# Layer two's output projection by pairs of tiles in seven products, and the copied sums made a stage earlier

## The chip, the cores and the metric

The kernel runs on one core of a Trainium2 chip. The core has a matrix engine (PE in the profile; its weight loads have a row of their own, PEld), a vector engine (DVE), a scalar engine (ACT), a general engine (POOL) and a queue engine (SP) that issues most of the transfers. Sixteen DMA engines carry the transfers, whoever issues them. Matmuls write to PSUM, which has eight banks of 128 partitions by 512 fp32 values; all else is held in SBUF or in DRAM.

The metric is the device time of one execution, in microseconds (us). The text calls the matrix multiplications of a 128 by 128 weight block with a block of up to 512 columns "matmuls", and gives their width in columns.

## What is computed

The input is x, 2048 rows of 512 values. Two layers of the same form follow each other; each has an attention block A and a gated block B, both with a layer norm before them and a residual sum behind:

```python
x = x + _A_ref(_layernorm(x), A_wqkv, A_wo)      # linear attention, 32 heads
x = x + _B_ref(_layernorm(x), B_w_in, B_w_sp, B_b_sp, B_w_out)
x = x + _A_ref(_layernorm(x), A_wqkv, A_wo)
x = x + _B_ref(_layernorm(x), B_w_in, B_w_sp, B_b_sp, B_w_out)

def _B_ref(x, w_in, w_sp, b_sp, w_out):
    z = gelu(x @ w_in)                            # 2048 x 1792
    z1, z2 = z[:, :896], layernorm(z[:, 896:])
    g = w_sp @ z2 + b_sp[:, None]                 # w_sp: 2048 x 2048
    return (z1 * g) @ w_out                       # w_out: 896 x 512
```

All of it is fp32. Where the kernel multiplies, it splits each operand into a high part, rounded to the matrix engine's fp32r type, and a low part, the rest; a product is then three matmuls: high by high, high by low, low by high.

## The kernel before

One program does both layers (L = 0 and L = 1); engine queues run in the order in which the kernel's text issues instructions (a manual schedule), and semaphores make each instruction wait for what it reads and overwrites. SBUF is handed out in named slots: 22 pages (`pg`, 128 by 512), 6 quads (`qd`, 2048 columns), 4 bigs (`bg`, 3584 columns) and sixteen z tiles; PSUM in 8 banks. A slot that is given back goes to the end of a queue, and its next user waits for the last reader.

Each layer has three classes. **P1** reads the rows in 16 tiles of 128, normalises them, turns them by a store to DRAM (`xt`) and a load back, and makes the projections K and Q and the attention sums. **P2** finishes attention, adds the residual, stores x, and makes gelu(x @ w_in), z2 in the z tiles and z1 in DRAM. **P4** multiplies by w_sp, gates with z1, and multiplies by w_out.

P4's product with w_sp is cut by Strassen-like sums into seven parts, done in the order P2, P1, P6, P7, P4, P5, P3. A part has eight steps; a step splits 128 by 1024 values of w_sp or of sums of w_sp into high and low (`wsp`: ACT L932, then DVE L933) and runs 18 or 24 matmuls of width 512 (L1098 to L1100). Layer one's P4 and layer two's P2 and P4 are divided once more, into seven products with two steps each (14 steps of 12 matmuls). Sums of w_sp blocks for the divided parts lie in DRAM (`hP`). They are made by transfers alone (`Sums.halve`): a copy by SP's queue (L835) and an accumulating transfer by POOL's queue (L839), 32 in all. The first 16 (numbers 0 to 15, for "P4") are issued in layer one's P4, one a step, at steps g = 10 to 25 (its parts P1, P6 and the first two steps of P7). The other 16 (numbers 16 to 31, for layer two's "P2") are issued in layer two's P1: eight copies in its steps s = 2 to 9, eight accumulating transfers in its steps s = 6 to 13.

The result g of the spatial product stands in the four bigs, transposed: feature block f (seven of 128) by 512 rows. When a part has finished a block, `evac` (DVE) moves it from PSUM and `gate` multiplies it by z1 in place, on POOL (L1136). z1 comes back from DRAM by loads that run three ahead (`ask`).

The output stage is `for i in range(NT)` at the end of `P4.run`. For each of 16 row tiles it makes seven blocks of 128 by 128 high and low (`zsplit`: ACT L127 and DVE L130, 128 by 896 values), then 21 matmuls of width 512 (`o`, through `mm3` at L141 to L143) into one bank, adds the bank to the residual x that was loaded from DRAM (DVE L1206) and stores the sum (L1208). The high and low parts of w_out are made in P3 (`wpiece`, one of seven blocks of 128 by 512 a step), in the z tiles that P3 no longer needs.

Of the kernel before, what the change touches and what calls it, by code (L numbers as in the profile page):

```python
# [11 lines left out]
F32R = mybir.dt.float32r  # L12
AF = mybir.ActivationFunctionType
OP = mybir.AluOpType

P = 128
# [3 lines left out]
NT = S // P  # L20
NCHK = S // 512
NF = FH // P
HF = FH // 2
HT = NT // 2
# [28 lines left out]
DIVIDED = (("P4",), ("P2", "P4"))  # L53


class Sheets:


# [16 lines left out]
def mixer_kernel(ctx: ExitStack, tc: tile.TileContext, x_in, wqkv, wo_d, win1_d, win2_d, wsp_d, bsp_d, wout_d,  # L75
                 ident_d, mask_d, out_d):
    nc = tc.nc
    consts = ctx.enter_context(tc.tile_pool(name="consts", bufs=1))
    main = ctx.enter_context(tc.tile_pool(name="main", bufs=1))
# [5 lines left out]
    pages = Slots(main, "pg", 22)  # L85
# [20 lines left out]
    nc.vector.memset(mhalf, -0.5)  # L106

    xs = {(0, i): x_in[i * P:(i + 1) * P, :] for i in range(NT)}
    for st in (1, 2, 3):
        for i in range(NT):  # L110
            xs[st, i] = dram.tile(PAGE, F32, name=f"x{st}_{i}")
    for i in range(NT):
        xs[4, i] = out_d[i * P:(i + 1) * P, :]
    z1s = {}

    def load(ap, slots=pages):
        t = slots.get(PAGE)
        nc.sync.dma_start(t, ap)
        return t

    def behind(ins, other):

        tc.add_manual_dep(ins.ins, other.ins.name, mybir.DependencyInfo(
            mybir.DependencyClass.Sync, mybir.DependencyReason.DATA))

    def high(h, src):
        nc.scalar.activation(h, src, AF.Copy)  # L127
# [153 lines left out]
    class P1:  # L281
# [181 lines left out]
        def run(self, sums):  # L463
            side = deque([self.win2] * NF)
            ND = NT - DEFER
            for s in range(1, NT + 2):
                self.loadx(s + 3)
                self.turn.load(s + 1)
                if 2 <= s < NT:
                    self.T_high(s)  # L470
                if s == 1:
                    if not self.kb:
                        self.K(0)
                    self.K(1)
                elif 2 < s <= NT:
                    self.K(s - 1)
                self.ln_a(s + 2)
                if 2 <= s < NT:
                    self.T_low(s)
                if s <= NT:  # L480
                    self.K_phi(s - 1)
                if s <= ND:
                    self.Q(s - 1)
                if s == NT + 1:
                    self.late()
                if s <= NT:
# [386 lines left out]
    class P4:  # L873
# [8 lines left out]
        def __init__(self, p2, sums):  # L882
            self.L = p2.L
            self.p2, self.sums = p2, sums
            self.raw, self.w, self.z, self.z1, self.x, self.zs = {}, {}, {}, {}, {}, {}
            self.div = DIVIDED[self.L]
            self.steps = []
            for p in self.ORDER:
                if p in self.div:
                    self.steps += [(p, 2 * r + q) for r in range(7) for q in range(2)]  # L890
                else:
                    self.steps += [(p, k) for k in range(HT)]
            self.tmp, self.bank = {}, {}
            self.made = 0
# [244 lines left out]
        def evac(self, p):  # L1139

            V, bs = nc.vector, self.bs
            gates = []
            for j in range(2):
# [55 lines left out]
        def o(self, i):  # L1199
# [10 lines left out]
            if i % 4 == 3:  # L1210
                bigs.put(self.gb[i // 4])

        def zahead(self, g):

            while self.zmade <= g:
                self.zsum(self.zmade + 1)
                self.zpart(self.zmade)
                self.zmade += 1

        def run(self, nxt):  # L1220
# [16 lines left out]
            for g in range(n):  # L1237
# [11 lines left out]
                    self.evac(p)  # L1249
                    self.sp(g + 2)  # L1250
                self.sums.tick()
                if nxt is not None and 10 <= g < 26:
                    self.sums.halve(g - 10, self.mark)
                if g == 3 and not self.div:
                    self.loadb()
                if p in self.div:
# [8 lines left out]
                    self.ask(3)  # L1265
                self.tick()
                if p == "P3":
                    if k < NF:
                        self.wpiece(k)
                    if k == 6:  # L1270
                        self.loadx(0)
                        self.loadx(1)
                    if k == 7:
                        self.zsplit(0)
                if p == "P7" and k == HT - 1 and self.div:
                    self.sp(g + 3)
                if k == HT - 1 and not evac_first:
                    self.evac(p)
# [76 lines left out]
```

## Time and profile before

| | us |
|---|---|
| median of three executions | 1381.27 |
| the three executions | 1381.01, 1381.27, 7891.05 |
| the profiled execution, its own time | 1382.98 |
| its span, from the first to the last instruction | 1381.2 |
| PE busy in the span | 1371.3 |
| layer two's part P3, about | 1268.5 to 1301.2 |
| layer two's output stage, about | 1301.2 to 1377.4 |

A row of the profile that describes a group of instructions names the line in the kernel, the engine, the operation, what is written and read, the shape and the count; behind the bar stand the busy time in us and the mean duration of one in ns, and then the idle time of the engine ahead of them and what ended it. A row of a timeline begins with the start and the duration in us, and x3 means that three such instructions are merged. A row of windows has for each engine the busy time in that stretch and, in brackets, the number of instructions begun. Matmuls overlap each other's fill and drain, so a matmul's recorded duration is longer than the distance to the next one; this text calls that distance the spacing.

### The profile page before, as it was taken

The page shows a single profiled execution, that of the slowest core. Times are in us where ns is not written, and L with a number is a line of the kernel's source. Part 1 is how long each engine was busy: PE and PEld are TensorE (multiplying, and loading weights), DVE is VectorE, ACT ScalarE, POOL GpSimd, SP SyncE. Part 2 cuts the span into 40 slices and gives each one's busy share as a digit, 9 for nine tenths or more (in the row PEclk, how much of TensorE's full clock was granted, in tenths as well). Part 3 has the DMA queues.
Part 4 walks back from the last instruction along what each step waited for, and adds up shares of the span by engine and source line. Part 5 has one row for each costly group of instructions (what it writes and reads, how often), then busy time and mean ns, then how long its engine had stood idle before and what let it go on. Part 6 is the DMA issues. An engine that isn't in the chain of part 4 may idle for free.

```text
span 1381.2 us, 17464 instructions
## 1 busy us (share of the span) xinstructions
PE 1371.3 (99%) x6158; PEld 1144.6 (83%) x6158; DVE 914.2 (66%) x1371; ACT 599.8 (43%) x919; POOL 418.6 (30%) x506
## 2 busy tenths in 40 slices
PE   9999999999999999999999999999999999999998
PEld 7888888888888888888888778888888888888887
DVE  6665877753575689684566658775437768887732
ACT  5764534434332364251366545433345333643410
POOL 3753355543441300351023434432100022023500
PEclk9999999999999999999999999999999999999999
DMA  5873268775986956453648932564346444464432
GB/s 179 267 242 93 92 193 271 247 241 187 346 281 223 269 162 205 138 194 125 226 138 235 234 102 92 169 189 161 121 130 207 150 164 150 152 192 152 160 123 91
DMA packets 149977, 251.91 MB, mean 182 GB/s; under 512 B 12545, under 2 KB 51201, under 8 KB 149633
## 3 DMA queue, kind: packets, MB, share of 16 engines
q1 hardware_dynamic: 147584, 242.40, 53.9%
q0 software_dynamic: 2304, 8.39, 3.3%
q8 instruction: 48, 0.79, 0.2%
q14 instruction: 41, 0.33, 0.1%
HBM read 182.85 MB, written 84.67 MB: 194 GB/s over the span
## 4 chain that ended last, share of the span: by engine, by line
PE 95%; DMA 3%; DVE 1%; ACT 1%; issue 0%; SPq 0%; ACTq 0%; DVEq 0%
PE bank L141 19%; PE bank L143 19%; PE bank L142 19%; PE bank L1100 12%; PE bank L1099 12%; PE bank L1098 12%; DMA pg<-xt 1%; DMA qd<-s 1%; PE bank L229 1%; PE bank L558 1%; PE bank L569 0%; DMA xt<-pg 0%; PE bank L441 0%; DVE qd L933 0%; DVE bg L1153 0%
## 5 line engine op out<-in xcount | busy, mean ns | idle before, releaser
L1098 PE MATMUL bank<-qd,pg 128*128 128x512 f32 x776 | 302.0, 389 | 0.5 <-ACT pg L970 0.5
L1100 PE MATMUL bank<-qd,pg 128*128 128x512 f32 x776 | 302.1, 389 | 0.0
L1099 PE MATMUL bank<-qd,pg 128*128 128x512 f32 x776 | 302.0, 389 | 0.0
L933 DVE TENSOR_TENSOR qd<-qd,qd 128x1024 fp32r<-128x1024 f32 x130 | 166.3, 1280 | 124.2 <-ACT qd L932 123.8
L1136 POOL TENSOR_TENSOR bg<-bg,pg 128x512 f32<-128x512 f32 x56 | 104.9, 1883 | 400.3 <-ACT qd L932 330.2
L932 ACT ACTIVATE qd<-qd 128x1024 fp32r<-128x1024 f32 x130 | 137.2, 1056 | 178.0 <-PE bank L1100 121.3
L1098 PEld LDWEIGHTS bank<-qd,pg 128*128 128x128 f32 x776 | 145.7, 188 | 31.2 <-ACT pg L970 0.9
L1099 PEld LDWEIGHTS bank<-qd,pg 128*128 128x128 f32 x776 | 145.7, 188 | 30.8 <-DVE qd L933 0.4
L1100 PEld LDWEIGHTS bank<-qd,pg 128*128 128x128 f32 x776 | 145.7, 188 | 30.3 <-DVE pg L972 0.5
L143 PE MATMUL bank<-qd,pg 128*128 128x512 f32 x384 | 150.0, 391 | 0.0
L217 ACT ACTIVATE pg<-pg,nb,rs 128x512 f32<-128x512 f32 x63 | 51.1, 812 | 177.0 <-POOL nb L211 176.5
L208 POOL TENSOR_SCALAR rs<-mv 128x1 f32<-128x1 f32 x96 | 27.3, 285 | 331.7 <-DVE mv L206 325.7
L141 PE MATMUL bank<-qd,pg 128*128 128x512 f32 x288 | 112.6, 391 | 0.4 <-DVE pg L130 0.4
L142 PE MATMUL bank<-qd,pg 128*128 128x512 f32 x288 | 112.3, 390 | 0.0
L141 PE MATMUL bank<-bg,qd 128*128 128x448 f32 x256 | 94.1, 368 | 0.7 <-ACT qd L127 0.7
L142 PE MATMUL bank<-bg,qd 128*128 128x448 f32 x256 | 93.6, 366 | 0.0
L143 PE MATMUL bank<-bg,qd 128*128 128x448 f32 x256 | 93.5, 365 | 0.1
L143 PE MATMUL bank<-qd,bg 128*128 128x512 f32 x224 | 87.4, 390 | 0.0
L142 PE MATMUL bank<-qd,bg 128*128 128x512 f32 x224 | 87.4, 390 | 0.0
L141 PE MATMUL bank<-qd,bg 128*128 128x512 f32 x224 | 87.2, 389 | 0.0
L141 PE MATMUL bank<-wo,qd 128*128 128x512 f32 x224 | 87.1, 389 | 0.0
L142 PE MATMUL bank<-wo,qd 128*128 128x512 f32 x224 | 87.1, 389 | 0.0
(136 smaller groups left out, 2598.8 us busy)
## 6 DMA issues: line engine op xcount, KB each, us to landing
qd<-s SPq DMA_DIRECT2D x64, 512.0 KB, 3.6
qd<-in_wsp_dram SPq DMA_DIRECT2D x42, 512.0 KB, 4.2
pg<-x SPq DMA_DIRECT2D x64, 256.0 KB, 3.0
z<-pg SPq DMA_DIRECT2D x56, 256.0 KB, 2.8
pg<-z SPq DMA_DIRECT2D x56, 256.0 KB, 4.1
x<-pg SPq DMA_DIRECT2D x48, 256.0 KB, 2.6
pg<-in_wsp_dram SPq DMA_DIRECT2D x48, 256.0 KB, 4.8
s<-pg SPq DMA_DIRECT2D x48, 256.0 KB, 4.2
```

The source lines that it names most:

```text
L141: nc.tensor.matmul(out, ah, bh, start=start, stop=False)
L142: nc.tensor.matmul(out, ah, bl, start=False, stop=False)
L143: nc.tensor.matmul(out, al, bh, start=False, stop=stop)
L208: nc.gpsimd.tensor_scalar(rs, mv[:, 1:2], LN_EPS, None, op0=OP.add)
L217: nc.scalar.activation(y, x, AF.Identity, bias=nb, scale=rs)
L229: nc.tensor.transpose(b[:, c, :], src[:, c * P:(c + 1) * P], ident)
L932: self.mark = nc.scalar.activation(w[:, 0], r, AF.Copy)
L933: nc.vector.tensor_sub(w[:, 1], r, w[:, 0].bitcast(F32))
L1098: m(out, h[:, o], w[:, 0, j, :], start=start, stop=False, skip_group_check=True)
L1099: m(out, h[:, o], w[:, 1, j, :], start=False, stop=False, skip_group_check=True)
L1100: m(out, l[:, o], w[:, 0, j, :], start=False, stop=stop, skip_group_check=True)
L1136: behind(nc.gpsimd.tensor_tensor(u, u, z1, op=OP.mult), self.mark)
```

## The change

Layer two's output stage is replaced; layer one's stays. The new stage, `out7`, takes row tiles in pairs. With the six feature blocks 0 to 5 in two groups of three, the pair's rows are a 2 by 2 block matrix (tile by group), w_out's rows and column halves (256 wide) are another, and their product is made by seven products instead of eight (`omul`, 9 matmuls of width 256 each). Feature block 6 is multiplied as before (`olone`: six matmuls of width 256 and three of width 512). Partial sums are combined in PSUM: ACT copies one bank's half into another (three copies of 256 columns a pair) and DVE adds a copied part twice, and later matmuls accumulate on top. The sums of the left operand are made by DVE in the bigs (`osum`, four of 128 by 384), its high and low parts by ACT and DVE (`ohigh`, `olow`: 384, 768, 256 and 1536 columns), one pair ahead. Sums and splits of w_out are made in P5 and P3 (`wseven`).

For the first seven pairs the residual isn't loaded: P2's x is stored straight to the output tensor (`xs[3]` is now `xs[4]`), ACT copies the finished banks to pages, and POOL issues an accumulating transfer into the output (`ofinish`). The last pair is added on DVE and stored by SP (`olast`).

In layer two the gates with f > 2 of the first two row chunks, and those with f > 3 of the others, run on DVE instead of POOL. Of P3's last results one half is moved from PSUM before the output stage, the other half behind the first pair's work. The copied and accumulated sums 16 to 31 move from layer two's P1 to layer one's P4: seven copies at the even steps of its divided part P4, one at its last step, and the eight accumulating transfers at the steps of P5.

```diff
+FIRST = 6
+PARTS = {("P1", k): k - 2 for k in range(2, 8)} | {("P6", k): 6 + k for k in range(8)}
+PARTS |= {("P7", 0): 14, ("P7", 1): 15} | {("P4", 2 * k): 16 + k for k in range(7)}
+PARTS |= {("P4", 13): 23} | {("P5", k): 24 + k for k in range(8)}
...
-        xs[4, i] = out_d[i * P:(i + 1) * P, :]
+        xs[3, i] = xs[4, i] = out_d[i * P:(i + 1) * P, :]
...
-                elif 2 <= s < 10:
-                    sums.halve(14 + s, None)
-                if self.L == 1 and 6 <= s < 14:
-                    sums.halve(18 + s, self.mark)
...
-            behind(nc.gpsimd.tensor_tensor(u, u, z1, op=OP.mult), self.mark)
+            if self.L == 1 and f > 2 and (n < 2 or f > 3):
+                nc.vector.tensor_mul(u, u, z1)
+            else:
+                behind(nc.gpsimd.tensor_tensor(u, u, z1, op=OP.mult), self.mark)
...
+        def omul(self, parts, r, out, start, stop):
+            h, l, q = parts
+            for f in range(3):
...
+                m(out, A, x, start=start and f == 0, stop=False, skip_group_check=True)
+                m(out, A, y, start=False, stop=False, skip_group_check=True)
+                m(out, B, x, start=False, stop=stop and f == 2, skip_group_check=True)
...
+        def ofinish(self, i, *parts):
+            y = pages.get(PAGE)
+            for b, c in parts:
+                nc.scalar.activation(y[:, c], b, AF.Copy)
+            nc.gpsimd.dma_start(xs[4, i], y, accum_op=OP.add)
+            pages.put(y)
+
+        def olast(self, i, b, c):
+            x = self.x[i]
+            nc.vector.tensor_add(x[:, c], x[:, c], b)
+            nc.sync.dma_start(xs[4, i][:, c], x[:, c])
+
+        def first(self):
+            self.opart(0)
+            self.ohigh(0, 1, 2)
+            self.olow(0, 1)
+            self.osum(1, 3, 2, 4)
+            self.ohigh(3)
+            self.olow(3, 2)
+
+        def pair(self, j):
+            z, u = self.zs.pop(j), banks.get(PAGE)
+            self.omul(z, 1, u[:, 0:256], True, False)
+            y = banks.get(PAGE)
+            nc.scalar.activation(y[:, 0:256], u[:, 0:256], AF.Copy)
+            return u, y, z
+
+        def out7(self):
...
+                if more:
+                    self.opart(j + 1)
+                    self.ohigh(0, 1, 2)
+                    self.olow(0, 1, 2)
+                    if j:
+                        self.omul(z, 2, u[:, lo], False, True)
+                    self.omul(z, 5, u[:, hi], False, True)
...
+                    nc.scalar.activation(c, u[:, hi], AF.Copy)
+                    self.osum(1, 3)
...
+                self.omul(z, 6, y[:, lo], False, False)
+                nc.scalar.activation(d[:, lo], y[:, lo], AF.Copy)
+                if more:
+                    up, yp, zp = self.pair(j + 1)
...
+                V.tensor_add(y[:, lo], y[:, lo], c)
+                if more:
+                    self.osum(2, 4)
+                    self.ohigh(3)
+                self.omul(z, 7, d[:, lo], False, False)
+                V.tensor_add(d[:, hi], d[:, lo], c)
...
+                if more:
+                    self.olow(3)
+                if j == 0:
+                    self.evac("P3", (1,))
+                for _ in range((0, 1, 2, 2, 1)[j] if j < 5 else 0):
+                    self.tick()
+                self.omul(z, 3, y[:, lo], False, True)
+                if more:
+                    self.omul(z, 4, d[:, lo], False, True)
...
+                self.olone(j, 0, u[:, lo], lo)
+                self.olone(j, 0, y[:, lo], hi)
+                self.olone(j, 1, d)
+                if more:
+                    self.ofinish(2 * j, (u[:, lo], lo), (y[:, lo], hi))
+                    self.ofinish(2 * j + 1, (d, slice(0, 512)))
...
-                if nxt is not None and 10 <= g < 26:
-                    self.sums.halve(g - 10, self.mark)
+                if nxt is not None:
+                    self.sums.halve(PARTS.get((p, k), -1), self.mark)
...
+                    if nxt is None:
+                        if k == FIRST:
+                            self.first()
...
+                if nxt is None:
+                    self.wseven(p, k)
...
+            if nxt is None:
+                self.out7()
+                return
```

More of the change, by code (lines that the diff above doesn't have):

```diff
@@ L893, in __init__ @@
             self.tmp, self.bank = {}, {}
+            self.ones = {}
+            self.wz = deque(WZ)
             self.made = 0
@@ L1211, in o, with wraw, wsums @@
                 bigs.put(self.gb[i // 4])
+        def wraw(self, *fs):
+            self.traw = [load(wout_d[f * P:(f + 1) * P, :]) for f in fs]
+        def wsums(self):
+            V = nc.vector
+            a, b = self.traw
+            s, t = self.tsum = pages.get([P, 2, 256]), pages.get([P, 2, 256])
+            lo, hi = slice(0, 256), slice(256, 512)
+            V.tensor_sub(s[:, 0], a[:, hi], a[:, lo])
+            V.tensor_sub(t[:, 0], b[:, hi], a[:, hi])
+            V.tensor_sub(s[:, 1], b[:, hi], s[:, 0])
+            V.tensor_sub(t[:, 1], b[:, lo], s[:, 1])
@@ new lines, in wtiles, with wparts @@
+        def wtiles(self, shape):
+            return [main.tile(shape, F32R, tag=f"z{n}", bufs=1, name=f"wo{self.L}_{n}")
+                    for n in (self.wz.popleft(), self.wz.popleft())]
+        def wparts(self, f):
+            (a, b), (s, t) = self.traw, self.tsum
+            B = self.wout
+            if f == 0:
+                B[4] = self.wtiles([P, 3, 256])
+            B[0, f], B[1, f] = p, q = self.wtiles([P, 3, 256]), self.wtiles([P, 3, 256])
+            split(p[0][:, 0], p[1][:, 0], a[:, 0:256])
+            split(p[0][:, 1:3], p[1][:, 1:3], b.rearrange("p (n w) -> p n w", n=2))
+            split(q[0][:, 0:2], q[1][:, 0:2], s)
+            split(q[0][:, 2], q[1][:, 2], t[:, 0])
+            split(B[4][0][:, f], B[4][1][:, f], t[:, 1])
+            pages.put(*self.traw, *self.tsum)
@@ new lines, in wlone, with wseven, opart @@
+        def wlone(self):
+            h, l = self.wout[6] = self.wtiles(PAGE)
+            split(h, l, self.traw[0])
+            pages.put(*self.traw)
+        def wseven(self, p, k):
+            at = (p, k)
+            if at in WRAW:
+                self.wraw(*WRAW[at])
+            if at in WSUM:
+                self.wsums()
+            if at in WPART:
+                self.wparts(WPART[at])
+            if at == WLONE:
+                self.wlone()
+        def opart(self, j):
+            n, k = divmod(2 * j, 4)
+            h, l = (quads.get([P, 15, P], F32R) for _ in range(2))
+            q = quads.get([P, 2, 3, 256], F32R)
+            self.zs[j] = h, l, q
+            self.ones[j] = pages.get([P, 2, 256], F32R)
+            g = self.gb[n][:, :, k * P:(k + 2) * P]
+            t = self.ones[j]
+            self.op = g[:, 0:3, 0:P], g[:, 3:6, 0:P], g[:, 0:3, P:], g[:, 3:6, P:]
+            s = [x[:, 0:12].rearrange("p (u t) c -> p u (t c)", u=6) for x in (h, l)]
+            self.osplits = [(h[:, 12:15], l[:, 12:15], g[:, 0:3, 0:P]), (q[:, 0], q[:, 1], g[:, 3:6]),
+                            (t[:, 0], t[:, 1], g[:, 6]), (*s, g[:, 0:6])]
@@ new lines, in ohigh, with olow, osum @@
+        def ohigh(self, *ms):
+            for m in ms:
+                h, l, s = self.osplits[m]
+                high(h, s)
+        def olow(self, *ms):
+            for m in ms:
+                h, l, s = self.osplits[m]
+                low(l, s, h)
+        def osum(self, *ms):
+            a11, a12, a21, a22 = self.op
+            V = nc.vector
+            for m in ms:
+                if m == 1:
+                    V.tensor_add(a22, a21, a22)
+                elif m == 3:
+                    V.tensor_sub(a21, a11, a21)
+                elif m == 2:
+                    V.tensor_sub(a11, a22, a11)
+                else:
+                    V.tensor_sub(a12, a12, a11)
@@ new lines, in olone @@
+        def olone(self, j, i, out, c=slice(0, 512)):
+            t = self.ones[j]
+            a, b = (t[:, k, i * P:(i + 1) * P] for k in range(2))
+            x, y = (w[:, c] for w in self.wout[6])
+            m = nc.tensor.matmul
+            m(out, a, x, start=False, stop=False, skip_group_check=True)
+            m(out, a, y, start=False, stop=False, skip_group_check=True)
+            m(out, b, x, start=False, stop=True, skip_group_check=True)
+        def ofinish(self, i, *parts):
[4 more added lines that the diff above has]
+            pages.put(y)
@@ new lines, in out7 @@
+        def out7(self):
+            V = nc.vector
+            lo, hi = slice(0, 256), slice(256, 512)
+            last = HT - 1
+            u, y, z = self.pair(0)
+            for j in range(HT):
+                if j == last - 1:
+                    self.loadx(NT - 2)
+                    self.loadx(NT - 1)
+                d, s = banks.get(PAGE), pages.get(PAGE)
+                c = s[:, lo]
+                more = j < last
+                if more:
[6 more added lines that the diff above has]
+                    if j == 0:
+                        self.omul(z, 2, u[:, lo], False, True)
+                    nc.scalar.activation(c, u[:, hi], AF.Copy)
+                    self.osum(1, 3)
+                else:
+                    self.omul(z, 2, u[:, lo], False, True)
+                self.omul(z, 6, y[:, lo], False, False)
+                nc.scalar.activation(d[:, lo], y[:, lo], AF.Copy)
+                if more:
+                    up, yp, zp = self.pair(j + 1)
+                else:
+                    self.omul(z, 5, u[:, hi], False, True)
+                    nc.scalar.activation(c, u[:, hi], AF.Copy)
+                V.tensor_add(y[:, lo], y[:, lo], c)
[4 more added lines that the diff above has]
+                V.tensor_add(d[:, hi], d[:, lo], c)
+                pages.put(s)
+                if more:
+                    self.olow(3)
+                if j == 0:
+                    self.evac("P3", (1,))
[4 more added lines that the diff above has]
+                    self.omul(z, 4, d[:, lo], False, True)
+                    quads.put(*z)
+                self.olone(j, 0, u[:, lo], lo)
[4 more added lines that the diff above has]
+                    self.ofinish(2 * j + 1, (d, slice(0, 512)))
+                    banks.put(u, y, d)
+                    pages.put(self.ones.pop(j))
+                    u, y, z = up, yp, zp
+            self.omul(z, 4, d[:, lo], False, True)
+            self.olast(NT - 2, u[:, lo], lo)
+            self.olast(NT - 2, y[:, lo], hi)
+            self.olast(NT - 1, d[:, hi], hi)
+            self.olast(NT - 1, d[:, lo], lo)
```

29 lines of the change are left out of this document (22 added, 7 removed).

## The prediction

> **What bounds the kernel now.** I read the engines' busy time first, then the chain that ended last, then the windows of layer two's end.
>
> ```profile
> PE 1371.3 (99%) x6158; PEld 1144.6 (83%) x6158; DVE 914.2 (66%) x1371; ACT 599.8 (43%) x919; POOL 418.6 (30%) x506
> PE 95%; DMA 3%; DVE 1%; ACT 1%; issue 0%; SPq 0%; ACTq 0%; DVEq 0%
> ```
> ```profile
> 1268.50:1301.20 32.70, 32.70 (x146) 27.08 (x145) 28.96 (x30) 17.04 (x24) 18.54 (x10) 1.00 0.60 201
> 1301.20:1377.40 76.20, 76.20 (x337) 62.90 (x335) 27.75 (x32) 10.51 (x11) 6.09 (x5) 1.00 0.32 104
> ```
> PE is the whole chain but for a few breaks. In the output stage (second window) it never rests: 336 matmuls of the kernel's text (16 tiles by 21) in 76.2 us, a spacing of 0.2268, so 42 x 0.2268 = **9.53 us** for two tiles. DVE is busy there 28 of 76 us, but 29 of 32.7 in P3 just before. So the change is worth what it takes off PE, unless another engine makes PE wait.
>
> **The change part by part.**
>
> *Matmul widths.* A pair now has 63 + 6 = 69 matmuls of width 256 and three of 512: 19,200 columns instead of 21,504, 10.7% fewer, but 72 instructions and weight loads instead of 42. All hangs on the spacing at width 256. No warm stream of them is in the trace. Recorded durations and spacings of other shapes:
>
> ```profile
> L141 PE MATMUL bank<-wo,qd 128*128 128x512 f32 x112 | 43.6, 389 | 0.0
> L142 PE MATMUL bank<-bg,qd 128*128 128x448 f32 x256 | 93.6, 366 | 0.0
> L558 PE MATMUL bank<-qd,qd 128*128 128x128 f32 x64 | 7.5, 275 | 0.0
> ```
> ```profile
> 211.70 0.37 PE L142 MATMUL bank<-bg,qd 128*128 128x448 f32 x1
> ...
> 216.16 0.36 PE L143 MATMUL bank<-bg,qd 128*128 128x448 f32 x1
> ```
> ```profile
> 131.20 3.57 PE bank L558 x32
> ```
> ```profile
> L441 PEld LDWEIGHTS bank<-pg,ones x14: 263/334/338, 2.3 to 8.0; 128*128 128x128 f32 x14
> L441 PE MATMUL bank<-pg,ones x14: 280/632/797, 2.3 to 8.2; 128*128 128x512 f32 x10, 128*128 128x256 f32 x4
> ```
> ```profile
> 7.82 0.69 PE L441 MATMUL bank<-pg,ones 128*128 128x256 f32 x3
> ```
> Width 448: 4.46 us over 22 steps (23 rows) is 0.203, and 366 - 203 = 163 ns. Width 512: 389 - 227 = 162. Plain fp32 at 128: 3.57/32 = 0.112, and 275 - 112 = 163. So spacing is the recorded duration less 163 ns, for all three. The shortest of the start-up's idle matmuls (L441), which can only be one of its four of width 256, took 280: spacing **0.117**. Bounds: 0.112 below, which the 32 matmuls of L558 kept up with a new weight load each; above, the straight line through 448 and 512, 0.227 - 4 x 0.024 = 0.130. I take 0.117, the one row of this width and type. A pair is then 69 x 0.117 + 3 x 0.227 = **8.75 us**; gain 0.78, for eight pairs **6.2 us** (at 0.112: 9.0; at 0.130: a loss of 1.0).
>
> A rule to weigh: the Trainium skill, "TensorE: Matmul & The Clock Gate", section "Back-to-back issue gap", gives N/2.4 + 2.5 ns for a warm matmul of N columns, so 109 ns here and 216 at 512. The trace has 227 at 512, 11 more, so I don't use it; by it the estimate would be a gain of 8 x 0.89 = 7.1 us.
>
> *Work beside it.* Costs of the shapes, one each:
>
> ```profile
> L1019 DVE TENSOR_TENSOR pg<-z_z,pg 128x256 fp32r<-128x256 f32 x24 | 9.0, 418 | 0.0
> L972 DVE TENSOR_TENSOR pg<-pg,pg 128x384 fp32r<-128x384 f32 x16 | 8.9, 558 | 0.0
> L933 DVE TENSOR_TENSOR qd<-qd,qd 128x1024 fp32r<-128x1024 f32 x130 | 166.3, 1280 | 124.2 <-ACT qd L932 123.8
> L1015 ACT ACTIVATE pg<-z_z 128x256 fp32r<-128x256 f32 x36 | 12.7, 403 | 0.0
> L932 ACT ACTIVATE qd<-qd 128x1024 fp32r<-128x1024 f32 x130 | 137.2, 1056 | 178.0 <-PE bank L1100 121.3
> ```
> DVE a pair: lows of 384, 768, 256 and 1536 (0.56, 0.99, 0.42, 1.85 by the slope of these rows), four sums of 384 (2.23), two adds of 256 (0.84): 6.9 us. ACT: highs (0.51, 0.85, 0.40, 1.49) and six copies, five of 256 and one of 512 (2.6): 5.9. Both fit beside 8.75, so throughput doesn't bind. The waits do more: each must be covered by matmuls queued between.
>
> ```profile
> 1377.16 0.39 PE L143 MATMUL bank<-wo,qd 128*128 128x512 f32 x1
> 1377.58 0.69 DVE L1206 TENSOR_TENSOR pg<-pg,bank 128x512 f32<-128x512 f32 x1 [4.07 <-PE bank L143]
> ```
> A handover costs 0.03 us after the recorded end, which lies 0.16 behind the spacing. Product 3 waits for product 6, ACT's copy and DVE's add: 0.16 + 0.03 + 0.40 + 0.03 + 0.42 + 0.03 = 1.07, while PE has the next pair's product 1 and product 7 to do, 18 x 0.117 = 2.1: covered. Product 4 waits for DVE's add behind product 7: 0.16 + 0.03 + 0.42 + 0.03 = 0.64, covered by product 3 alone, 1.05. The 0.4 to spare is less than one sum of 384 (0.56) that DVE may be in, or one gate; behind this add stand `olow`(1536), gates and the next pair's lows. Product 5 of the next pair needs that low part: the add frees DVE about 6.0 after the pair's start, ACT's 1536 is done at 7.1, DVE's at 8.9, needed at 8.75 + 1.05 = 9.8. I allow 0.15 a pair, **+1.0** (0 to 4).
>
> *The switch.* P3's DVE gains sums and splits of w_out, eight gates (0.6 each) and `first`. By the walk of its queue (P5's eight moves 5 us, eight splits 1.6 with the z part, w_out 7.5, gates 5, `first` 7) it ends near 32, with PE's end of P3 at 32.6 and product 5 a microsecond later. That is thin, but POOL's gates, beside which DVE ran slower, are gone: nothing (0 to 2).
>
> *End.* The last add is 256 wide instead of 512: -0.27, and the last pair, with nothing queued between, waits 0.1: **-0.2**. The last accumulating transfer is issued two POOL issues after the seventh pair; if it landed as these, it would end with the last store, seven products and 2 us later:
>
> ```profile
> hP<-hP POOLq DMA_DIRECT2D x8, 512.0 KB, 7.6
> out_dram<-pg SPq DMA_DIRECT2D x16, 256.0 KB, 2.0
> ```
>
> *The moved sums.* In layer two's P1, PE stops twice for the load of turned x:
>
> ```profile
> 790.96 0.39 PE L143 MATMUL bank<-pg,pg 128*128 128x512 f32 x1
> 792.80 0.50 PE L141 MATMUL bank<-qd,z_h 128*128 128x512 f32 x1 [1.45 <-ACT z_h L127]
> 793.13 0.40 PE L142 MATMUL bank<-qd,z_h 128*128 128x512 f32 x1
> 793.52 0.50 PE L143 MATMUL bank<-qd,pg 128*128 128x512 f32 x1
> ```
> ```profile
> 803.89 0.39 PE L143 MATMUL bank<-pg,pg 128*128 128x512 f32 x1
> 805.08 0.50 PE L141 MATMUL bank<-qd,z_h 128*128 128x512 f32 x1 [0.80 <-ACT z_h L127]
> ```
> ```profile
> 783.96 7.40 DMA pg<-xt
> ```
> ```profile
> 782.49 0.92 POOL L839 DMA_DIRECT2D hP<-hP  x1
> ...
> 787.98 0.94 POOL L839 DMA_DIRECT2D hP<-hP  x1
> ```
> ```profile
> DMA to landing us min/median/max: 2.5/2.8/5.2
> ```
> Lost: 1.84 - 0.23, 1.19 - 0.23, and behind each two late matmuls (0.72 instead of 0.45): 3.1 us. The load took 7.40 with two accumulating transfers in the queues; at the same step of layer one (last row, the xt transfers from 94 to 106 us), beside the same large weight load, the longest took 5.2 and PE didn't stop. These transfers leave: **-3.1** (0 to -3.1). What they did where they were dense, in layer one's P6:
>
> ```profile
> q0 software_dynamic: 436, 1.59, 51.5%
> qd<-s SPq DMA_DIRECT2D x3, 512.0 KB, 9.7
> ```
> ```profile
> 454.19 11.52 DMA qd<-s
> ```
> Loads landed after 10 us and more, and PE lost about 0.8 at P7's start. Now they come in P5, one in 5.44 us instead of 4.08, with loads issued four steps (22 us) ahead; P3 follows with the same shape of queue. I put half of that price: **+0.4** (0 to 1.7). SP's copies stand in a part whose loads lead by four steps of 2.7 us: nothing.
>
> **Sum**: -6.2 + 1.0 - 0.2 - 3.1 + 0.4 = **-8.1**. The profiled execution took 1382.98 (1.8 around its span), so 1374.9 of its kind; it stands 1.7 over the median shown, 1381.27, from which I get **1373**.
>
> **The rivals.**
> *Half the width isn't half the time.* At 0.130 the pairs lose 1.0 instead of gaining 6.2: 1380. The line through 448 and 512 speaks for it; the 280 ns against.
> *Slower: the weight load shows.* If a load can't run under a short matmul, as after each wait above (792.80 to 793.13 was a spacing of 0.33, 0.11 more), 69 matmuls take 0.228 each: 16.4 a pair, +55 instead of -6.2, 1434. From 0.135 on the kernel is slower. Against it: L441's cold stream, (0.69 - 0.28)/2 = 0.205 apart with loads recorded at 0.33, so loads overlap each other and the matmuls. The Trainium skill, same page, section "The mechanism" says that loads overlap matmuls in flight only for different row groups; by that rule this rival would hold, and the trace disagrees: 227 ns is less than a stream and a load in turn, 213 + 107 by the page's figures.
> *DVE sets the pace.* Product 4 late by one sum (0.5) in seven pairs, and 1.5 at the switch: +4 instead of +1.0, 1377.
> *The moved sums bring nothing*: P1's stops stay, and layer one pays 1.7: 1373 + 3.1 + 1.3 = 1377.5.
>
> **How the numbers follow.** Forecast (1370 to 1376) 0.55; wide spacing (1378 to 1383) 0.13; DVE 0.13; moved sums 0.11; spacing 0.112 with no waits (1369) 0.05; loads that show 0.03. The range 1367 to 1382 leaves out the last and half of the second. Two per cent (27 us) is about what a measurement of this kernel can tell from no change; only the shown loads pass it: slower 0.03, faster 0.01.
>
> **What would show it.** Right: L-lines of `omul` recorded near 280 ns with PE busy without breaks, pairs 8.8 us apart; no stop of PE near 790 and 804; product 4 behind DVE's add by tenths at most. Wrong: a recorded duration near 293 or more, DVE named as what PE waits for in most pairs, or a stop at layer one's P3.

## The result, and the profile after

The changed kernel takes **1375.25 us** (median of five runs, 1374.89 to 1375.83) beside 1381.81 for the kernel before, a ratio of 0.9953 with a 95% interval of 0.9937 to 0.9969. The 1381.81 is the median of four executions; a fifth, which took 7891.05, is left out. Later runs of both in one set gave 1374.92 and 1382.11, a ratio of 0.9948 (0.9935 to 0.9961). The change is clear of noise and half a per cent. The traced execution has a span of 1373.1 against 1381.2, 8.1 less.

The page's row of engines, and then the same windows as before the change: layer two's P3, its output stage, the tail.

```profile
PE 1365.2 (99%) x6398; PEld 1152.9 (84%) x6398; DVE 948.0 (69%) x1458; ACT 629.1 (46%) x989; POOL 399.9 (29%) x506
```
```profile
1263.90:1296.67 32.77, 32.77 (x146) 27.12 (x145) 30.54 (x50) 16.24 (x27) 0.00 (x0) 1.00 0.45 145
1296.67:1369.28 72.61, 72.15 (x577) 70.74 (x575) 53.36 (x87) 38.96 (x73) 12.18 (x14) 1.00 0.43 69
1369.28:1373.10 3.82, 0.10 (x1) 0.00 (x0) 0.75 (x2) 0.00 (x0) 0.00 (x0) 1.00 0.26 87
```

P3 takes what it took (32.8 against 32.7), although DVE is busy for 30.5 of it. The output stage takes 72.6 instead of 76.2. In it PE rests 0.46, all of it at one place, which the timeline of PE shows: the first pair's product 1 ends, and product 5 waits for ACT's copy of product 1. The spacing there is 0.74 instead of 0.12, and 0.22 behind it.

```profile
1297.62 0.28 PE L1328 MATMUL bank<-wo,qd 128*128 128x256 f32 x1
1298.36 0.39 PE L1326 MATMUL bank<-wo,qd 128*128 128x256 f32 x1 [0.46 <-ACT bank L1364]
1298.58 0.28 PE L1327 MATMUL bank<-wo,qd 128*128 128x256 f32 x1
...
1314.97 0.28 PE L1335 MATMUL bank<-wo,pg 128*128 128x256 f32 x1
...
1323.94 0.28 PE L1335 MATMUL bank<-wo,pg 128*128 128x256 f32 x1
```

The last two rows are the same matmul of two neighbouring pairs: a pair takes 8.97 us. The group of the new matmuls, by shape:

```profile
L1326 PE MATMUL bank<-wo,qd 128*128 128x256 f32 x168 | 47.7, 284 | 0.5 <-ACT bank L1364 0.5
L1328 PE MATMUL bank<-wo,qd 128*128 128x256 f32 x168 | 47.5, 283 | 0.0
```

A recorded 283 ns, which less 163 is a spacing of **0.120**; with it 69 narrow matmuls and three wide ones of 0.23 make the 8.97.

In layer two's P1, the window around the two former stops, in the kernel before and after (the last figures are the granted clock, the DMA share and GB/s):

```profile
785.00:809.00 24.00, 21.75 (x92) 16.48 (x92) 12.30 (x20) 11.33 (x20) 7.18 (x9) 1.00 0.74 198
```
```profile
785.00:809.00 24.00, 24.00 (x107) 19.87 (x107) 13.43 (x21) 12.43 (x22) 7.51 (x8) 1.00 0.42 139
```

PE doesn't rest there any more, and the DMA share fell from 0.74 to 0.42. In layer one PE has a new stop, near the end of P3:

```profile
614.32 0.39 PE L1108 MATMUL bank<-qd,pg 128*128 128x512 f32 x1
615.15 0.50 PE L1109 MATMUL bank<-qd,pg 128*128 128x512 f32 x1 [0.44 <-DVE pg L981]
```

The chain of waits leads from it back to P3's first load of w_out, which took 9.31 (the loads before the change took 4.3 to 5.0). The last accumulating transfer, issued 1.8 us ahead of that load, was in the queues for most of that time:

```profile
581.70 0.82 POOL L846 DMA_DIRECT2D hP<-hP  x1 [4.61 <-ACT qd L941]
```
```profile
583.53 9.31 DMA pg<-in_wout_dram
```

That alone doesn't make PE stop: in the second trace of the changed kernel the same load took 9.07, and PE has no stop there.

| term (us, from the two traces) | forecast | measured |
|---|---|---|
| widths of the output stage's matmuls | -6.2 | -4.4 (8 x (9.52 - 8.97)) |
| waits inside the new stage | +1.0 | +0.8 (0.72 at the first pair, 0.1 at the last) |
| tail behind the last matmul | -0.2 | 0.0 |
| switch from P3 | 0 | 0 |
| layer two's P1 (from the same matmul ahead of the stops to the same one behind them) | -3.1 | -3.6 |
| layer one, by the moved sums | +0.4 | +0.7 |
| stops of the first trace near 40, 48 and 476, absent in the second | not in the sum | -1.6 |
| **sum** | **-8.1** | **-8.1** |

The sums agree, but not for the reasons forecast: the output stage with its tail gave 1.8 less, and 1.6 came from stops that the forecast had left alone. The experiments ask which of these terms belong to the change.

### The profile page after: what moved, and what is told of

It is laid out like the page before. It is cut to its first block, busy times and chain, and to the rows that moved or that the text cites. A ratio compares the mean times of both kernels' runs of the same rounds, so it can differ in the third digit from the quotient of the medians.

```text
span 1373.1 us, 18095 instructions
## 1 busy us (share of the span) xinstructions
PE 1365.2 (99%) x6398; PEld 1152.9 (84%) x6398; DVE 948.0 (69%) x1458; ACT 629.1 (46%) x989; POOL 399.9 (29%) x506
## 4 chain that ended last, share of the span: by engine, by line
PE 93%; DVE 2%; DMA 1%; ACT 1%; issue 1%; POOL 1%; SPq 0%; DVEq 0%; POOLq 0%; ACTq 0%
PE bank L154 17%; PE bank L152 17%; PE bank L153 17%; PE bank L1109 12%; PE bank L1108 12%; PE bank L1107 12%; PE bank L1326 1%; PE bank L1327 1%; PE bank L1328 1%; DMA pg<-in_wout_dram 1%; PE bank L565 1%; PE bank L576 1%; PE bank L240 0%; DVE st L215 0%; DMA pg<-in_wsp_dram 0%
## 5 line engine op out<-in xcount | busy, mean ns | idle before, releaser
L1109 PEld LDWEIGHTS bank<-qd,pg 128*128 128x128 f32 x776 | 145.6, 188 | 31.2 <-DVE pg L981 0.9
L1108 PEld LDWEIGHTS bank<-qd,pg 128*128 128x128 f32 x776 | 145.6, 188 | 30.6 <-DVE qd L942 0.4
L1107 PEld LDWEIGHTS bank<-qd,pg 128*128 128x128 f32 x776 | 145.6, 188 | 30.1
L1148 POOL TENSOR_TENSOR bg<-bg,pg 128x512 f32<-128x512 f32 x42 | 75.5, 1804 | 276.6 <-ACT qd L941 224.1
L154 PEld LDWEIGHTS bank<-qd,pg 128*128 128x128 f32 x384 | 72.1, 188 | 15.5 <-DVE pg L141 0.4
L856 POOL TENSOR_TENSOR pg<-pg,pg 128x512 f32<-128x512 f32 x48 | 68.4, 1425 | 37.5 <-DMA pg<-in_wsp_dram 21.8
```

The lines of the kernel that those rows point to most:

```text
L154: nc.tensor.matmul(out, al, bh, start=False, stop=stop)
L856: nc.gpsimd.tensor_tensor(t, a, b, op=OP.add)
L1107: m(out, h[:, o], w[:, 0, j, :], start=start, stop=False, skip_group_check=True)
L1108: m(out, h[:, o], w[:, 1, j, :], start=False, stop=False, skip_group_check=True)
L1109: m(out, l[:, o], w[:, 0, j, :], start=False, stop=stop, skip_group_check=True)
```

## The experiments

**The two parts apart, and the trace of before a second time.** First the moved sums are put back into layer two's P1:

```diff
-PARTS |= {("P7", 0): 14, ("P7", 1): 15} | {("P4", 2 * k): 16 + k for k in range(7)}
-PARTS |= {("P4", 13): 23} | {("P5", k): 24 + k for k in range(8)}
+PARTS |= {("P7", 0): 14, ("P7", 1): 15}
...
+                elif 2 <= s < 10:
+                    sums.halve(14 + s, None)
+                if self.L == 1 and 6 <= s < 14:
+                    sums.halve(18 + s, self.mark)
```

> The changed kernel with sums 16 to 31 back in layer two's P1, as before. If the moved sums were worth what the two traces show (P1's stops -3.4, a new stop at the end of layer one's P3 +0.6), it is 2.8 slower than the changed kernel: about 1378.0, with PE's stops back near 790 and 804 and none near 614. If the stops of the first trace were chance, it stays at 1375.3. The output stage stays at 72.6 in both.

Measured: 1377.90 (median of 11), 0.9976 of before (0.9967 to 0.9985). PE's stops near 790 and 803 are back, and there is none near 614:

```profile
790.94 0.50 PE L151 MATMUL bank<-qd,z_h 128*128 128x512 f32 x1 [1.16 <-ACT z_h L137]
802.98 0.50 PE L151 MATMUL bank<-qd,z_h 128*128 128x512 f32 x1 [0.52 <-ACT z_h L137]
```

Then the kernel before with the same move alone (the table PARTS, and the two branches of P1 taken out):

> The kernel before with only sums 16 to 31 moved to layer one's P4 and P5. If the moved sums work alone: 2.8 below the kernel before, about 1379, ratio 0.998, without the stops near 790 and 804 and with the one near 615. If they bring nothing: ratio 1.000.

Measured: 1377.89 (median of 11), 0.9974 of before (0.9966 to 0.9983): 3.7 less than the 1381.58 of that set, where 2.8 was expected; the interval is 2.3 to 4.7, so it doesn't exclude 2.8. P1's stops are gone. The new stop in layer one stands at another place, at the end of the divided part P4, and is larger, 1.5 with its followers (the traced execution took 1379.98, 2.1 over the median):

```profile
543.86 0.50 PE L1099 MATMUL bank<-qd,pg 128*128 128x512 f32 x1 [0.98 <-ACT pg L971]
```

So each part alone is worth about 3.7: 1381.58 - 1377.90 for the output stage with all that comes with it, 1381.58 - 1377.89 for the moved sums. Together that would be 7.4, and the changed kernel has 6.6 and 7.2 less than the runs of before beside it.

> The kernel before, unchanged, for a second trace. If PE's stops near 40, 48 and 476, which the changed kernel's trace lacks, vary by execution, at least one of them is missing or of another size here, while those near 790 and 804 stay. If the change took them away, all five are here as in the first trace.

The second trace of the unchanged kernel has a span of 1378.2, not 1381.2. PE's stops near 40, 48 and 476 are missing in it; those of P1 are there, with the same releaser:

```profile
790.19 0.50 PE L141 MATMUL bank<-qd,z_h 128*128 128x512 f32 x1 [1.15 <-ACT z_h L127]
802.20 0.50 PE L141 MATMUL bank<-qd,z_h 128*128 128x512 f32 x1 [0.47 <-ACT z_h L127]
```

The stop near 476 (about 1 us in all) turns up in eight of the thirteen traces of this document's kernels, with the sums moved and without. It is no part of the change. P1's stops are there in all four traces of kernels with the sums in P1 (3.0 to 3.6 in all), and in none of the nine without them.

**The price of half the width alone**, in layer two's output stage of the kernel before:

```diff
-                mm3(b, (q[:, 0, f, :], q[:, 1, f, :]), self.wout[f], f == 0, f == NF - 1)
+                if self.L == 0:
+                    mm3(b, (q[:, 0, f, :], q[:, 1, f, :]), self.wout[f], f == 0, f == NF - 1)
+                    continue
+                m = nc.tensor.matmul
+                for c in (slice(0, 256), slice(256, 512)):
+                    wh, wl = (t[:, c] for t in self.wout[f])
+                    first = f == 0 and c.start == 0
+                    m(b[:, c], q[:, 0, f, :], wh, start=first, stop=False, skip_group_check=True)
+                    m(b[:, c], q[:, 0, f, :], wl, start=False, stop=False, skip_group_check=True)
+                    m(b[:, c], q[:, 1, f, :], wh, start=False, stop=f == NF - 1, skip_group_check=True)
```

> The kernel before with each matmul of layer two's output stage cut into two of width 256, nothing else: 672 matmuls instead of 336, the same columns. At the 0.120 that the changed kernel's trace shows, 80.6 instead of 76.2: +4.4, about 1386. At the 0.117 of the prediction: +2.4. At 0.130: +11. If weight loads showed (0.228): +77. If the 0.120 came from waits in the new stage and the bare spacing is half of 0.227, 0.1135: +0.1.

Measured: 1386.39, 1.0038 of before (1.0024 to 1.0052), +4.8. In its trace the 672 matmuls stand in a window without any rest of PE:

```profile
1300.00:1380.60 80.60, 80.60 (x673) 80.58 (x671) 26.91 (x32) 10.49 (x11) 6.07 (x5) 1.00 0.30 99
```

That is 0.120 each, from a stage with none of the new waits. So 0.120 is the spacing itself. By the line through 0.1200 at 256 and 0.2268 at 512, a column costs 0.417 ns and a matmul 13 ns on top of its columns. Two points always give a line; at 448 columns, with other operands, it gives 0.200 where the trace of before has 0.203. With that, a pair's 19,200 columns and 72 matmuls make 8.0 + 1.0, and before 21,504 columns and 42 matmuls made 9.0 + 0.6: the seven products save 0.96 of columns and pay back 0.40 in count. The line says nothing on whether the 13 ns are the weight load's or the matmul's.

**The cover of product 4**, that is, the matmuls that PE has still to do while DVE makes what product 4 waits for. The forecast gave the add behind product 7 a slack of 0.4 us, less than one sum of 384. In the trace of the changed kernel, DVE's row of that add in the third pair, and PE's row of product 4 (the first matmul of nine):

```profile
1321.56 0.56 DVE L1310 TENSOR_TENSOR bg<-bg 128x384 f32<-128x384 f32 x1
1322.03 0.42 DVE L1405 TENSOR_TENSOR bank<-bank,pg 128x256 f32<-128x256 f32 x1
```
```profile
1322.86 0.28 PE L1326 MATMUL bank<-wo,qd 128*128 128x256 f32 x1
```

The add ends at 1322.45 and product 4 begins 0.4 later, and so it is in all six pairs from the second to the seventh. DVE comes to the add straight from a sum. Two runs spend the slack, with one and with two sums whose result nobody reads:

```diff
+            idle = pages.get([P, 3, P])
...
                     self.osum(2, 4)
                     self.ohigh(3)
+                    for _ in range(1):
+                        V.tensor_add(idle, self.op[0], self.op[1])
...
                 V.tensor_add(d[:, hi], d[:, lo], c)
```

> The changed kernel with one idle sum of 128x384 (0.56 us on DVE) ahead of the add behind product 7, in each of the seven pairs that prepare another. DVE then has about 7.5 us of work in a pair of 8.97. If product 4's cover is 0.4 us, as the prediction has it and the trace shows, it is late by 0.16 and an exposed weight load of 0.1 in each: about +1.8, 1377.0. If DVE's total is what counts: nothing, 1375.3.

Measured: 1376.97, +1.7 on 1375.25. The two medians are from different sets of runs; the traces compare more closely: from the first matmul of the output stage to the last it is 74.45 instead of 72.43, +2.0. PE's weight load now waits for that add (0.24 and 0.10 in each of six pairs; the first pair has more room):

```profile
1323.07 0.42 DVE L1408 TENSOR_TENSOR bank<-bank,pg 128x256 f32<-128x256 f32 x1
1323.55 0.19 PEld L1326 LDWEIGHTS bank<-wo,qd 128*128 128x128 f32 x1 [0.29 <-DVE bank L1408]
```

> As the last, with two idle sums. By the cover of 0.4: late by 0.75 and the weight load of 0.1, seven times, so about +5.9, 1381.2. By the total (8.0 of 8.97 us): nothing, 1375.3.

Measured: 1381.18, +5.9 by the medians; the stage takes 78.55 in the trace, +6.1. A wait of 0.84 and 0.10 in each of six pairs, half of it in the first:

```profile
1324.84 0.43 DVE L1408 TENSOR_TENSOR bank<-bank,pg 128x256 f32<-128x256 f32 x1
1325.32 0.19 PEld L1326 LDWEIGHTS bank<-wo,qd 128*128 128x128 f32 x1 [0.88 <-DVE bank L1408]
```

DVE had time over in both runs (it is busy for 53.4 of 72.6 us without the extra sums, and they add 3.9 and 7.8), so its total doesn't decide. The order does: a sum that stands ahead of an add that PE waits for costs about all that passes 0.4.

**The gates on POOL again**, in layer two, as before the change:

```diff
-            if self.L == 1 and f > 2 and (n < 2 or f > 3):
-                nc.vector.tensor_mul(u, u, z1)
-            else:
+            if True:
                 behind(nc.gpsimd.tensor_tensor(u, u, z1, op=OP.mult), self.mark)
```

> The changed kernel with all of layer two's gates on POOL, as before. The prediction gave the switch into the output stage nothing because DVE runs faster without POOL beside it. If that cover is needed, DVE's operations in P3 take up to twice as long, DVE passes 32.8 us there, the first low parts are late, and PE stops ahead of product 1 or 5 for 2 to 4 us: 1377 to 1379. If the gates' place is of no account, because taking nine gates off DVE makes up for it: 1375.3 within 0.5.

Measured: 1383.46, 1.0015 of before (1.0006 to 1.0024): 8.2 slower than the changed kernel's 1375.25 of another set, and all its gain gone. Neither expectation had this. The run moves 14 gates back to POOL, not nine: eight in P3 and six in the output stage. In the traces P3 loses only 0.7, and the output stage 8.0 (80.48 instead of 72.43 between its first and last matmul), in the second to the fifth pair. POOL makes the last six gates there, and the rows of the third pair show what DVE does meanwhile:

```profile
1320.21 4.55 DVE L141 TENSOR_TENSOR qd<-bg,qd 128x384 fp32r<-128x384 f32 x2 [0.91 <-ACT qd L138]
1320.63 2.83 POOL L1146 TENSOR_TENSOR bg<-bg,pg 128x512 f32<-128x512 f32 x2
```
```profile
1323.95 0.38 PE L1326 MATMUL bank<-wo,qd 128*128 128x256 f32 x1 [1.35 <-DVE qd L141]
```

The view of the tile qd gives the shortest, median and longest of its low parts between 1310 and 1360, in ns:

```profile
L141 DVE TENSOR_TENSOR qd<-bg,qd x15: 557/1758/3680, 1310.5 to 1359.7; 128x384 fp32r<-128x384 f32 x5, 128x768 fp32r<-128x768 f32 x5, 128x1536 fp32r<-128x1536 f32 x5
```

The low part of 128x384 alone took 3.68 of the 4.55 and ended 0.4 behind POOL's second gate. In the fifth pair, with one gate of 1.61 beside it, it took 2.47. The next pair's product 1 waits for it (PE's row above, 1.35). By groups over the stage (this kernel, then the changed one, in which POOL issues the same transfers but makes no gates):

```profile
L141 DVE TENSOR_TENSOR qd<-bg,qd 128x384 fp32r<-128x384 f32 x7 | 13.3, 1900 | 4.8 <-ACT qd L138 4.8
```
```profile
L141 DVE TENSOR_TENSOR qd<-bg,qd 128x384 fp32r<-128x384 f32 x7 | 3.9, 559 | 2.5 <-ACT qd L138 2.5
```

**The stops that are left.** Product 1 of the first pair is issued between the two halves of P3's last matmuls:

```diff
             for j in range(2):
+                if j and p == "P3" and last and self.L == 1:
+                    self.start = self.pair(0)
                 for f in range(3):
...
-            u, y, z = self.pair(0)
+            u, y, z = self.start
```

> The changed kernel with one edit: product 1 of the first pair between the two halves of P3's last matmuls. The bare wait for ACT's copy (0.62 and 0.10) goes, the rest stays: about 0.7 below the changed kernel, 1374.5. If it didn't matter, or the product were itself late in P3, no less than 1375.2.

Measured: 1374.19 (five runs), 0.9942 of before (0.9928 to 0.9956). The changed kernel has 1374.92 in the same set. The two intervals overlap, so the medians don't show the 0.7; the traces do: from the same matmul early in P3 to the last one it is 103.70 instead of 104.39. PE's rest at the first pair is gone from the trace; the window around it, changed kernel and this one:

```profile
1290.00:1300.00 10.00, 9.54 (x53) 8.17 (x52) 7.93 (x13) 3.33 (x5) 0.00 (x0) 1.00 0.18 54
```
```profile
1290.00:1300.00 10.00, 10.00 (x55) 8.69 (x54) 8.30 (x13) 3.69 (x6) 0.00 (x0) 1.00 0.06 8
```

Then the same edit, and another place for the moved sums:

```diff
-PARTS |= {("P7", 0): 14, ("P7", 1): 15} | {("P4", 2 * k): 16 + k for k in range(7)}
-PARTS |= {("P4", 13): 23} | {("P5", k): 24 + k for k in range(8)}
+PARTS |= {("P7", 0): 14, ("P7", 1): 15}
+COPIES = {k: 16 + k for k in range(8)}
+ADDS = {k + 2: 24 + k for k in range(8)}
...
                 self.zsplit(i + 2)
+                self.sums.halve(COPIES.get(i, -1), self.mark)
+                self.sums.halve(ADDS.get(i, -1), self.mark)
```

> The changed kernel with two edits: sums 16 to 31 in layer one's output stage (copies at its tiles 0 to 7, accumulating transfers at tiles 2 to 9), and product 1 of the first pair between the two halves of P3's last matmuls. If the stop at the end of layer one's P3 comes from the accumulating transfers in P5, it goes (-0.7), and where the copies make the load behind P4 late that goes too (0 to -1.5); if the stop of 0.6 at the first pair is the bare wait for ACT's copy, it goes with its weight load (-0.7). So about 1373.8, and P1's stops stay away. If the output stage of layer one can't carry the transfers, PE stops there or at layer two's first steps, and it stays at 1375 or is slower.

Measured: 1374.88, 0.9959 of before (0.9945 to 0.9972): nothing gained on the changed kernel. P3's stop and the first pair's are gone, but PE now stops three times, near 676, 681 and 686, 1.4 in all:

```profile
685.70 0.39 PE L154 MATMUL bank<-wo,qd 128*128 128x512 f32 x1
686.52 0.50 PE L155 MATMUL bank<-wo,qd 128*128 128x512 f32 x1 [0.44 <-DVE qd L142]
```

With a copy in each of the first eight tiles of 4.76 us and an accumulating transfer in each from the third to the tenth, the DMA engines have hardly a gap from 640 to 690, and the loads of x take 9.5 us to land, against 3.0 in the changed kernel, which has no such transfers there (first this kernel's row, from 640 to 690, then the changed one's, from 615 to 690):

```profile
pg<-x SPq DMA_DIRECT2D x13, 256.0 KB, 9.5
```
```profile
pg<-x SPq DMA_DIRECT2D x17, 256.0 KB, 3.0
```

> The changed kernel with the same edit, and sums 16 to 31 with copies in layer one's P5 and accumulating transfers at tiles 0 to 7 of its output stage, two tiles earlier than in the run before. If those of the run before stopped PE near 680 because the last of them met the first loads of the next layer, these stops (1.6) shrink to a few tenths: 1373.5 to 1374. If any accumulating transfer every 4.8 us fills the sixteen DMA engines, so that the loads of x come late, the stops come back in the output stage or earlier, and it is 1375 or more.

Measured: 1373.90 (five runs), 0.9942 of before (0.9929 to 0.9955). The first expectation's time and place hold: with the accumulating transfers two tiles earlier, PE doesn't rest between 610 and 690. Its reason isn't shown alone, because the copies left the output stage too:

```profile
610.00:690.00 80.00, 80.00 (x354) 66.24 (x354) 43.15 (x53) 21.22 (x27) 20.86 (x25) 1.00 0.74 207
```

This is the lowest median of all, 1.0 under the changed kernel beside it. The intervals of the two overlap, so the times alone don't prove it better; the stops that it lacks are shown.

> The changed kernel, unchanged, beside the two others, for a second trace. If the stops near 476 and 542 vary by execution, one of them may appear here; the spacing of 0.120, the wait of 0.7 at the first pair and product 4's cover of 0.40 are the same in every execution.

Measured: 1374.92, and a trace with a span of 1371.6. The wait of 0.72 at the first pair and the spacing of 0.120 are there again; the stop near 614 isn't, nor one near 542 or 476. So the moved sums' price in layer one is itself a matter of the execution: over the seven traces with the accumulating transfers in P5 it was 0.7, 1.5, 1.0, 0.0, 0.1, 0.8 and 0.0. The part of it near 542 is there in four of these seven and in none of the other six traces; the part near 614 in two of the seven and in none of the six.

## Why the prediction was right, and where it wasn't

*The time.* 1373 was forecast and 1375.25 and 1374.92 measured, inside the range of 1367 to 1382; the gain of 8.1 came out as 6.6 and 7.2. The intervals tell a change of 0.2% from none, so the two per cent that the prediction names is far too coarse.

*What bounds the kernel.* PE, throughout: each term of the measured table but the tail is a rest of PE or a change in its matmuls, and DVE, with 34 us more work, ends no rest of PE in the new stage.

*Matmul widths.* The step that was mis-sized. The rule (recorded duration less 163 ns) holds: 283 - 163 = 120. The row put into it was wrong. 280 was the shortest of the start-up's idle matmuls, and 283 is the mean of the 168 here. Three nanoseconds in 552 matmuls are 1.7 us, which is nearly the whole error of -6.2 for -4.4. By the prediction's own terms the kernel would be slower from a spacing of 0.132 on, not 0.135; 0.120 is well below both. The rival of 0.130 came from a line through 448 and 512; by the columns' price and the 13 ns, 448 should be 0.200, and its measured 0.203, extended over three more steps of 64, went astray. The rule from the Trainium skill, "TensorE: Matmul & The Clock Gate", section "Back-to-back issue gap", gives 109 ns where 120 was measured and 216 where 227 was: 11 ns short at both widths, so its slope is right and its constant isn't for this stream. The rival of shown weight loads, and by it the rule in the same page's section "The mechanism", is refuted by the 672 matmuls at 0.120, each with a weight load of its own. The same section also names a background weight buffer, for which it lets a load go ahead; no run here shows which way these loads take.

*Waits inside the stage.* The sum of 0.8 for 1.0 agrees, but by another place. The forecast spread 0.15 over each pair; six of the eight pairs have none, and the first has 0.72, because nothing is queued between its product 1 and the product behind ACT's copy. The forecast looked at the waits of a running pair and not at those of the first. The slack of product 4 was right (0.4), and so was its price: one and two sums more cost 2.0 and 6.1 in the traces (1.8 and 5.9 expected). The rival of DVE setting the pace has a slip of its sum: seven times 0.5 and 1.5 are 5.0, which gives its 1377, not the 4 that it names.

*The switch.* Nothing, as forecast. The reason given, that POOL's gates are gone from beside DVE, carries far more than the 0 to 2 set beside it: with the gates on POOL P3 loses 0.7 and the output stage 8.0, in the pairs rather than at the switch.

*End.* -0.2 was forecast, 0.0 measured. The forecast counted one add of 256 behind the last matmul; two stand there, and end together after 0.75, where the one of 512 took 0.69. The last two stores leave SP one behind the other, and the tail is 3.8 as before.

*The moved sums.* -3.1 for P1 was right (3.0 to 3.6 over the four traces with the sums there), shown by the run without the move and the one with the move alone. +0.4 in layer one was of the right size (0 to 1.5, mean 0.6), but partly by luck: it is half of the 0.8 at P7's start, and that is the stop near 476, which comes and goes. The stop at layer one's P3, which the prediction named as a sign of being wrong, came in two of seven traces. That SP's copies in P4 cost nothing doesn't hold in each execution: the run with the move alone lost 1.5 at that part's end. Taken together the move is worth more by its runs (3.7) than by the forecast (2.7); the interval of the runs (2.3 to 4.7) holds both, and the traces, with stops that vary by a microsecond, can't say whether there is a difference.

*What the forecast left out.* Stops that come and go between executions of one kernel: two traces of the kernel before differ by 3.0 us. That the forecast's sum met the difference of the two spans to the tenth, 8.1, is luck: the widths gave 1.8 too little, the tail 0.2, and layer one cost 0.3 more; against that stand 1.6 of such stops, 0.5 more from P1 and 0.2 less waiting.

## What to carry to other kernels

Half as wide isn't half as long: a product cut from eight to seven must save more columns than its added matmuls cost at 13 ns each, and here 0.40 of 0.96 us went back. Where PE waits for an add, what counts is which instruction stands in front of that add in its queue, and the slack can be read from one pair and tested by an idle instruction of known length. Before a stop in one trace is put into a sum, look for it in a second trace of the same kernel.

## What the runs showed of the hardware

A DVE subtraction with two inputs in SBUF got longer by about as much as POOL's gates beside it took: 0.56 us alone, 2.47 beside one gate of 1.61, 3.68 beside two that took 2.83 together. The Trainium skill, "SBUF — State Buffer", section "Who interferes with whom", says that a DVE instruction with two SBUF inputs contends with a GpSimd instruction that reads SBUF; the trace agrees. On PE's path that cost 8.0 us for six gates.

An accumulating transfer of 512 KB from DRAM to DRAM takes some 8 us in the queues, and the loads beside it wait. In P5 of layer one (546 to 584), before the change and after it:

```profile
qd<-s SPq DMA_DIRECT2D x7, 512.0 KB, 3.5
```
```profile
q0 software_dynamic: 1037, 3.79, 56.1%
...
qd<-s SPq DMA_DIRECT2D x8, 512.0 KB, 7.6
hP<-in_wsp_dram POOLq DMA_DIRECT2D x4, 512.0 KB, 8.2
hP<-hP POOLq DMA_DIRECT2D x4, 512.0 KB, 8.7
```

The same load of w_sp's sums lands after 7.6 us instead of 3.5. Some seven such transfers (3.8 MB), one every 5 us, take 56% of the time of sixteen DMA engines here. PE lost nothing between 547 and 584 in any of the seven traces, with w_sp's loads issued, by the prediction's count, four steps (22 us) ahead; what was lost stands near 542, at the end of P4, and near 614, at the end of P3.
